# A causal head-wise convolution with a wave token mixing on one NeuronCore: residual adds on GpSimd, conv bands from TensorE, GpSimd in written order, one weight load per matrix and quarter, two-bank PSUM tiles

## The chip, the cores and the metric

The kernel runs on one core of one Trainium2 chip. The engines are named as the profile names them: PE (TensorE, matmul), DVE (VectorE), ACT (ScalarE), POOL (GpSimd) and SP (SyncE). In this kernel POOL and SP issue the DMA transfers. The metric is device microseconds (us) of one launch; less is better.

## The reference

Eight sequences of 4224 tokens with 192 channels. A causal convolution with seven taps, whose weights are a softmax for each of eight heads, is followed by a token mixing with complex weights and a channel mixing; both mixings add residuals.

```
w = softmax(weight, axis=-1)                      # (8 heads, 7 taps)
x = einsum('hk,bskhg->bshg', w, windows(x, 7))    # causal, x is (8, 4224, 192)
theta = x @ w_theta                               # w_theta (192, 192)
zr, zi = x * cos(theta), x * sin(theta)
y = einsum('ts,bsd->btd', w_tok_r, zr) + einsum('ts,bsd->btd', w_tok_i, zi)
u = x + y                                         # w_tok_r, w_tok_i (4224, 4224)
out = u + relu(u @ w_ch)                          # w_ch (192, 192)
```

The token mixing is by far the largest part. The token matrices are read as float32 and used as float16; the output is float32.

## The kernel before

**Token mixing.** The sum over 4224 tokens is cut into 33 chunks of 128 tokens (four quarters of 32 tokens from four places of the sequence, `token` names the place). The output's 33 row tiles of 128 tokens are taken two at a time, 17 units. For each chunk and unit the 2x2 product of (real, imaginary) weights by (cos, sin) parts is done with seven products instead of eight: the weight tiles are called "11", "21" (real part of the first and the second row tile), "12", "22" (imaginary part) and the sums "S1" to "S4"; the data tiles of a chunk are Z11, Z21, Z22 and T1 to T4. These are the matmuls of L394, 22 in a run of eleven chunks, seven runs in a step.

**Steps.** At most eleven chunks are resident in SBUF. A step is one unit with the chunks of that time; there are 58 (steps 0 to 57). Chunks 0 to 10 are made in steps 0 to 4 while the first units begin; each chunk serves 17 steps. In steps 17 to 22 and again in 35 to 40 the eleven resident chunks are replaced one or two at a step; this text calls these the two regroups. A row tile's partial sum goes to DRAM (`part`, L407) after steps that are not its last, and comes back (L334, `load_rows`) in the later ones. Steps 41 to 57 are final for their rows; of these 53 to 57 have fewer chunks and are called late.

**A chunk.** `load_chunk` makes a tile `xw` of inputs with a halo of earlier tokens: four loads on POOL (L177) and two copies from the chunk before on SP (L168). `conv` (L190) multiplies it with `bands`, matrices that hold the softmaxed taps, for a pair of heads a call; ACT copies the result out (L197) and SP stores the convolved x to DRAM as `xs` (L207). Then two `transpose` (six PE transposes L144, one ACT copy L148), four `theta` (PE L135, two ACT sines L226), `product` (DVE L231) and `sums` (DVE L237).

**Weights of a step.** `load_w` loads one named weight tile in four transfers, one a quarter (L289 on POOL), into a staging tile `st` with four buffers. `turn` (L301) transposes blocks of 32 on DVE from `st` to `wt`; `wsum` (L313) makes S1 to S4 on DVE.

**Residual.** `add_x` adds `xs` to the rows of a final step by a POOL transfer that accumulates (L347): into `pv`, the SBUF tile of the rows, or for late steps into `part` in DRAM, four steps ahead. `give` adds a finished run from PSUM to `pv` (ACT L357, DVE L359).

**Output.** `cast` makes a float16 copy `ub` of u on ACT, `turn_u` transposes it, `output` multiplies by w_ch and adds on DVE (L422), and SP stores (L428).

**Order.** `pe`, `dve` and `act` chain the instructions of their engine in the order in which the program writes them. Instructions on POOL and SP are not chained: the framework's scheduler places them. Each step has a list of events with due times in sevenths of the step ("units"); `mix` writes an event out when its matmuls reach that time. In step t: `turn` and `wsum` of step t+1 ("11" at 0.25, "21" 1.2, S3 2.05, "22" 2.2, S1 3.05, S2 3.3, "12" 4.2, S4 5.1), `load_rows` of t+1 at 1.6, `add_x` at 3.3 and 5.0, `load_w` of step t+2 at 0.3, 1.3, 2.3 and 4.3, and in the regroups `load_chunk` at 4.5 for chunks that start at t+2, and the twelve pieces of a chunk that starts at t+1 from 0.3 on (a second chunk 2.6 later).

**Start.** Before the first step POOL makes masks (L502, L504), from which DVE builds `bands` (L541 to L552), loads w_theta (L121 to L124), and issues x and weight loads. `idle` fills PE's early gaps with spare matmuls (L580).

**PSUM.** The tiles `y` of L394 take two banks, in two buffers. All others share the tag `mm`, one bank a tile in four buffers.

Of the kernel before, what the change touches and what calls it, by code (L numbers as in the profile page):

```python
# [10 lines left out]
ALU = mybir.AluOpType  # L11
# [5 lines left out]
def kernel(  # L17
# [69 lines left out]
    def act(ins):  # L87
        return in_order("act", ins)

    constp = ctx.enter_context(tc.tile_pool(name="const", bufs=1))  # L90
# [7 lines left out]
        tc.tile_pool(name="mmps", bufs=4, space=bass.MemoryType.PSUM)  # L98
# [7 lines left out]
    def bank(name, dtype=F32):  # L106
        return mmpool.tile([P, PC if dtype == F32 else 2 * PC], dtype,
                           name=name, tag="mm")
# [6 lines left out]
    ident = constp.tile([P, P], F16, name="ident")  # L115

    def channel_weights(w, name):
        R = D - P
        t = constp.tile([P, 4, D], F16, name=name)
        nc.vector.memset(t[:, 1:3, :], 0.0)  # L120
        nc.gpsimd.dma_start(out=t[:, 0, :], in_=w[0:P, :])  # L121
        nc.gpsimd.dma_start(out=t[0:R, 1, :], in_=w[P:D, :])
        nc.gpsimd.dma_start(out=t[R:P, 2, :], in_=w[0:R, :])
        nc.gpsimd.dma_start(out=t[:, 3, :], in_=w[R:D, :])  # L124
        return t
# [5 lines left out]
    def channel_mix(tT, k, w):  # L131
        v = bank("v")
        for b in range(2):
            for i in range(2):
                pe(nc.tensor.matmul(  # L135
                    v[:, b * D : (b + 1) * D], lhsT=tT[:, 3 * k + b + i, :],
                    rhs=w[:, 2 * b + i, :], start=(i == 0), stop=(i == 1),
                ))
        return v[:, 0 : 2 * D]

    def transposed(u):
        tp = bank("tp", F16)
        for k in range(6):
            pe(nc.tensor.transpose(  # L144
                tp[:, k * P : (k + 1) * P], u[:, k * P : (k + 1) * P], ident
            ))
        uT = wk.tile([P, 6, P], F16, name="uT", tag="uT")
        act(nc.scalar.activation(  # L148
            out=uT[:, :, :].rearrange("p k s -> p (k s)"), in_=tp[:, 0 : 6 * P],
            func=AT.Copy,  # L150
        ))
        return uT
# [3 lines left out]
    class Chunk:  # L156


        def __init__(self, k, before=None):
# [3 lines left out]
            for a in range(NQ):  # L163
# [13 lines left out]
                nc.gpsimd.dma_start(  # L177
                    out=self.xw[lo : lo + n, h, :, :],
                    in_=x[:, t0 : t0 + n, :].rearrange("b s d -> s b d"),
                )  # L180

        def conv(self, hp):
            if hp == 0:
                self.z = zpool.tile([P, 7, HN], F16, name="z", tag="z")
                self.x = self.z[:, T2 : T2 + 2, :].rearrange("p t n -> p (t n)")
            pc = bank("pc")
            for hh in range(2):
                h = 2 * hp + hh
                for half in range(2):
                    pe(nc.tensor.matmul(  # L190
                        pc[half * 2 * Q : (half + 1) * 2 * Q,
                           hh * B * G : (hh + 1) * B * G],
                        lhsT=bands[:, h, :, :].rearrange("p a m -> p (a m)"),
                        rhs=self.xw[:, half, :, h * G : (h + 1) * G],
# [4 lines left out]
                    :, :, hp * 2 * G : (hp + 1) * 2 * G  # L199
                ].rearrange("p b (h g) -> p h b g", h=2),  # L200
                in_=pc[:, 0 : 2 * B * G].rearrange("p (h b g) -> p h b g", h=2, b=B),
                func=AT.Copy,
            ))
            if hp == H // 2 - 1:
# [9 lines left out]
        def theta(self, g, k):  # L214
            v = channel_mix(self.xT[g], k, wth).rearrange(
                "p (b h e) -> p b h e", b=2, h=2
            )
            b0 = g * GB + 2 * k
            for first, bias in ((Z11, half_pi[:]), (Z21, None)):
                o = self.z[:, first : first + 2, :].rearrange(  # L220
                    "p h (b e) -> p b h e", e=HD
                )[:, b0 : b0 + 2, :, :]
# [18 lines left out]
        def tasks(self):  # L241

            for hp in (0, 2):
                yield lambda hp=hp: [self.conv(hp), self.conv(hp + 1)]
            for g in range(NG):
                yield lambda g=g: self.transpose(g)
            for g in range(NG):
                for k in range(2):
                    yield lambda g=g, k=k: self.theta(g, k)
# [17 lines left out]
    class Step:  # L267


        def __init__(self, t):  # L270
# [8 lines left out]
            self.blocks = ("11", "21", "22", "12") if self.pair else ("11", "12")  # L279
            self.st, self.w, self.ub, self.uT, self.pv = {}, {}, {}, {}, []  # L280

        def load_w(self, name):
            tb = self.tbs[int(name[0]) - 1]
            w = (moe_w_tok_r, moe_w_tok_i)[int(name[1]) - 1]
            st = wpool.tile([P, NQ, NW * Q], F16, name="st", tag="st", bufs=4)
            n = self.n * Q
            for a in range(NQ):
                t0 = token(self.ks[0], a)
                nc.gpsimd.dma_start(  # L289
                    out=st[a * Q : (a + 1) * Q, :, 0:n],  # L290
                    in_=w[tb * P : (tb + 1) * P, t0 : t0 + n]
                    .rearrange("(bt i) s -> i bt s", bt=NQ),
                )
            self.st[name] = st
# [4 lines left out]
        def turn(self, name):  # L299
# [3 lines left out]
                self.st[name][:, :, 0 : self.n * Q]  # L303
# [35 lines left out]
        def add_x(self, i):  # L339

            if self.late:
                to = part[(self.t // NU - 1) % 2][self.tbs[i], :, :]
            else:
                to = self.pv[i]
            rows = slice(self.tbs[i] * P, (self.tbs[i] + 1) * P)
            for cols in (slice(0, HN), slice(HN, N)) if self.late else (slice(0, N),):
                nc.gpsimd.dma_start(  # L347
                    out=to[:, cols], in_=xs[rows, cols], accum_op=ALU.add
                )
# [61 lines left out]
        def cast(self, i, g):  # L411
            self.ub[i, g] = wk.tile([P, GC], F16, name="ub", tag="ub", bufs=4)
# [7 lines left out]
        def output(self, i, g, k):  # L420
            pk = self.pv[i][:, g * GC + k * 2 * D : g * GC + (k + 1) * 2 * D]
            dve(nc.vector.scalar_tensor_tensor(  # L422
                out=pk, in0=channel_mix(self.uT[i, g], k, wch), scalar=0.0, in1=pk,
                op0=ALU.max, op1=ALU.add,
            ))
            if k == 1:
                rows = slice(self.tbs[i] * P, (self.tbs[i] + 1) * P)
                nc.sync.dma_start(  # L428
                    out=out[g * GB : (g + 1) * GB, rows, :].rearrange("b s d -> s b d"),
                    in_=self.pv[i][:, g * GC : (g + 1) * GC].rearrange(  # L430
                        "p (b d) -> p b d", d=D
                    ),
                )

        def outputs(self):
# [3 lines left out]
            for i in range(len(self.tbs)):  # L439
                at = ((-self.time / 7 + 0.6, 1.2) if late else (0.7, 12.7))[i]  # L440
                cast, turn, mix = (1, 2.6, 4.4) if late else (2, 3.6, 5.4)
                for g in range(NG):
# [3 lines left out]
                    for k in range(2):  # L446
                        found.append((d + mix + 0.7 * k,
                                      lambda i=i, g=g, k=k: self.output(i, g, k)))
# [8 lines left out]
    def step_events(t):  # L457
# [11 lines left out]
        if t + 2 < NSTEP:  # L469
            nxt = steps[t + 2]  # L470
            for j, name in enumerate(nxt.blocks):
                found.append(((0.3, 1.3, 2.3, 4.3)[j], lambda name=name: nxt.load_w(name)))
# [4 lines left out]
        if t >= NU - 2:  # L477
# [4 lines left out]
            for k in (k for k in range(NK) if start[k] == t + 1 and k >= NW):  # L482
                pos = [0, .5, 1.3, 1.5, 2.1, 2.3, 2.5, 2.7, 3.1, 3.15, 3.4, 3.6]
# [14 lines left out]
    spare = bank("spare")  # L498
    noise = zpool.tile([P, PC], F16, name="noise", tag="z")
    nc.vector.memset(noise, 0.0)  # L500
    masks = wk.tile([2 * WR, KS, 2, Q], F16, name="masks", tag="ub", bufs=4)
    nc.gpsimd.memset(masks, 1.0)  # L502
    for k in range(KS):
        nc.gpsimd.affine_select(  # L504
            out=masks[:, k, :, :], in_=masks[:, k, :, :], pattern=[[WR, 2], [1, Q]],
            channel_multiplier=-1, base=HALO - KS + 1 + k,
            compare_op=ALU.is_equal, fill=0.0,
# [3 lines left out]
    for a, lo in ((0, True), (1, False)):  # L511
# [4 lines left out]
        )  # L516
    wmax = constp.tile([P, H], F32, name="wmax")
# [150 lines left out]
```

## Time and profile before

| what | value |
|---|---|
| median of three runs | 1477.11 us (1475.83 to 1478.19) |
| the profiled execution | 1481.54 us, span 1479.8 us |
| mean granted PE clock | 0.996 |
| PE busy | 1435.6 us (97%) |
| DVE busy | 980.7 us (66%) |
| ACT busy | 385.9 us (26%) |
| POOL busy | 604.5 us (41%) |
| PE idle before L394, most of it for DVE L359 | 24.7 us (19.7) |
| POOL weight issues, L289 | 896 of 0.56 us, 88 KB each |
| POOL x issues, L177 | 132 of 0.594 us, 96 KB each |
| POOL residual issues, L347 | 24 into pv, 0.935 us; 18 into part, 1.217 us |
| moved by DMA | 281.96 MB |

The span is the time between the first and the last instruction of the profiled execution; it is 1.7 us under that execution's own time, which is itself 4.4 us above the median. Busy time of PE counts from the issue of a matmul to its modelled end, so that neighbours overlap: the 7656 matmuls of L394 have a mean of 327 ns each but follow each other about every 161 ns. "Idle before, releaser" is the time an engine stood still before an instruction and what ended it. The granted clock is a share of PE's full clock.

### The profile page before, as it was taken

The page shows a single profiled execution, that of the slowest core. Times are in us where ns is not written, and L with a number is a line of the kernel's source. Part 1 is how long each engine was busy: PE and PEld are TensorE (multiplying, and loading weights), DVE is VectorE, ACT ScalarE, POOL GpSimd, SP SyncE. Part 2 cuts the span into 40 slices and gives each one's busy share as a digit, 9 for nine tenths or more (in the row PEclk, how much of TensorE's full clock was granted, in tenths as well). Part 3 has the DMA queues.
Part 4 walks back from the last instruction along what each step waited for, and adds up shares of the span by engine and source line. Part 5 has one row for each costly group of instructions (what it writes and reads, how often), then busy time and mean ns, then how long its engine had stood idle before and what let it go on. Part 6 is the DMA issues. An engine that isn't in the chain of part 4 may idle for free.

```text
span 1479.8 us, 25342 instructions
## 1 busy us (share of the span) xinstructions
PE 1435.6 (97%) x10083; PEld 902.6 (61%) x10083; DVE 980.7 (66%) x1120; ACT 385.9 (26%) x664; POOL 604.5 (41%) x1096
## 2 busy tenths in 40 slices
PE   6899999999999999999999999998799999999997
PEld 3565666666666666666666666665466666666665
DVE  5885645454558787775666668778476667666676
ACT  5881111111135353000000015254021212222134
POOL 9743424242444542433324254553444333333330
PEclk9999999999999999999999999999999999999999
DMA  9997757464699999887868699999999989998675
GB/s 130 216 206 148 135 99 153 93 148 94 147 226 220 237 216 256 186 195 173 200 163 208 152 199 213 216 286 293 189 233 253 226 206 224 202 218 189 142 170 158
DMA packets 241318, 281.96 MB, mean 191 GB/s; under 512 B 76336, under 2 KB 209456, under 8 KB 241200
## 3 DMA queue, kind: packets, MB, share of 16 engines
q0 software_dynamic: 173280, 111.20, 54.0%
q1 hardware_dynamic: 67920, 169.14, 32.2%
q8 instruction: 79, 1.29, 0.3%
q14 instruction: 39, 0.32, 0.1%
HBM read 245.49 MB, written 108.13 MB: 239 GB/s over the span
## 4 chain that ended last, share of the span: by engine, by line
PE 84%; DMA 9%; POOL 4%; DVE 2%; issue 1%; ACT 0%; SPq 0%; DVEq 0%; POOLq 0%; ACTq 0%
PE y L394 77%; PE v L135 4%; DMA xw<-in_x_dram 3%; DMA st<-in_moe_w_tok_r_dram 3%; PE tp L144 2%; POOL st L289 2%; DMA st<-in_moe_w_tok_i_dram 2%; PE pc L190 1%; DMA part<-xs 1%; POOL xw L177 1%; DVE pv L359 1%; DMA xw<-xw 0%; DMA part<-pv 0%; DVE z L237 0%; DVE z L231 0%
## 5 line engine op out<-in xcount | busy, mean ns | idle before, releaser
L394 PE MATMUL y<-z,wt 128*128 128x384 f16 x7656 | 1312.1, 327 | 24.7 <-DVE pv L359 19.7
L394 PEld LDWEIGHTS <-wt 128*128 128x128 f16 x7656 | 738.1, 98 | 482.7 <-issue 31.5
L359 DVE TENSOR_TENSOR pv<-y,pv 128x768 f32<-128x768 f32 x324 | 308.9, 953 | 429.5 <-PE y L394 414.5
L289 POOL DMA_DIRECT2D st<-in_moe_w_tok_r_dram x448 | 244.2, 566 | 355.0 <-DVE wt L301 302.9
L289 POOL DMA_DIRECT2D st<-in_moe_w_tok_i_dram x448 | 243.7, 562 | 349.6 <-DVE wt L301 296.4
L301 DVE STREAM_TRANSPOSE wt<-st 128x1408 f16<-128x1408 f16 (+7 forms) x224 | 326.6, 1463 | 10.9 <-DMA st<-in_moe_w_tok_r_dram 8.5
L148 ACT ACTIVATE uT<-tp 128x768 f16<-128x768 f16 x132 | 105.5, 817 | 321.8 <-PE tp L144 321.8
L313 DVE TENSOR_TENSOR wt<-wt 128x1408 f16<-128x1408 f16 (+7 forms) x216 | 173.6, 804 | 10.1 <-PE y L394 6.6
L197 ACT ACTIVATE z<-pc 128x384 f16<-128x384 f32 x132 | 58.4, 504 | 384.2 <-PE pc L190 384.0
L357 ACT ACTIVATE pv<-y 128x768 f32<-128x768 f32 x66 | 53.8, 816 | 275.2 <-PE y L394 274.7
L135 PEld LDWEIGHTS <-uT 128*128 128x128 f16 x1056 | 93.4, 98 | 34.9 <-ACT uT L148 3.8
L177 POOL DMA_DIRECT2D xw<-in_x_dram x132 | 76.7, 594 | 50.5 <-DMA st<-in_moe_w_tok_r_dram 18.1
L422 DVE SCALAR_TENSOR_TENSOR pv<-v,pv 128x384 f32<-128x384 f32 x132 | 71.4, 548 | 24.5 <-PE v L135 24.0
L226 ACT ACTIVATE z<-v,half_pi 128x384 f16<-128x384 f32 x132 | 77.7, 589 | 32.3 <-PE v L135 31.2
L237 DVE TENSOR_TENSOR z<-z 128x768 f16<-128x768 f16 x132 | 73.6, 557 | 7.3 <-DMA xs<-z 2.4
L413 ACT ACTIVATE ub<-pv 128x768 f16<-128x768 f32 x66 | 52.2, 835 | 71.8 <-DVE pv L359 71.7
L135 PE MATMUL v<-wch,uT 128*128 128x192 f16 x528 | 63.8, 246 | 2.6 <-ACT uT L148 2.6
L231 DVE TENSOR_TENSOR z<-z 128x1536 f16<-128x1536 f16 x66 | 60.0, 950 | 9.1 <-ACT z L226 9.0
L226 ACT ACTIVATE z<-v 128x384 f16<-128x384 f32 x132 | 65.5, 497 | 0.0
L135 PE MATMUL v<-wth,uT 128*128 128x192 f16 x528 | 62.5, 248 | 0.8 <-ACT z L226 0.8
L347 POOL DMA_DIRECT2D pv<-xs x24 | 22.1, 935 | 71.6 <-ACT ub L413 29.3
L190 PE MATMUL pc<-xw,bands 96*64 96x192 f16 x528 | 35.4, 254 | 4.4 <-DMA xs<-z 1.9
(45 smaller groups left out, 195.3 us busy)
## 6 DMA issues: line engine op xcount, KB each, us to landing
part<-pv SPq DMA_DIRECT2D x79, 768.0 KB, 4.1
pv<-part SPq DMA_DIRECT2D x79, 768.0 KB, 6.5
out_dram<-pv SPq DMA_DIRECT2D x66, 384.0 KB, 4.5
st<-in_moe_w_tok_r_dram POOLq DMA_DIRECT2D x280, 88.0 KB, 5.1
st<-in_moe_w_tok_i_dram POOLq DMA_DIRECT2D x280, 88.0 KB, 3.9
pv<-xs POOLq DMA_DIRECT2D x24, 768.0 KB, 6.8
xs<-z SPq DMA_DIRECT2D x132, 96.0 KB, 4.6
xw<-in_x_dram POOLq DMA_DIRECT2D x121, 96.0 KB, 4.8
```

The lines of the kernel that those rows point to most:

```text
L135: pe(nc.tensor.matmul(v[:, b * D : (b + 1) * D], lhsT=tT[:, 3 * k + b + i, :], rhs=w[:, 2 * b + i, :], start=(i == 0), stop=(i == 1),))
L148: act(nc.scalar.activation(out=uT[:, :, :].rearrange("p k s -> p (k s)"), in_=tp[:, 0 : 6 * P], func=AT.Copy,))
L177: nc.gpsimd.dma_start(out=self.xw[lo : lo + n, h, :, :], in_=x[:, t0 : t0 + n, :].rearrange("b s d -> s b d"),)
L226: act(nc.scalar.activation(**args))
L231: dve(nc.vector.tensor_tensor(out=o, in0=xv, in1=o, op=ALU.mult))
L237: dve(nc.vector.tensor_tensor(out=z[:, o, :], in0=z[:, a, :], in1=z[:, b, :], op=ALU.subtract))
L289: nc.gpsimd.dma_start(out=st[a * Q : (a + 1) * Q, :, 0:n], in_=w[tb * P : (tb + 1) * P, t0 : t0 + n] .rearrange("(bt i) s -> i bt s", bt=NQ),)
L301: dve(nc.vector.transpose(self.w[name][:, 0 : self.n, :, :], self.st[name][:, :, 0 : self.n * Q] .rearrange("p bt (c j) -> p c bt j", j=Q),))
L313: dve(nc.vector.tensor_tensor(out=self.w[name][:, 0 : self.n, :, :], in0=self.w[a][:, 0 : self.n, :, :], in1=self.w[b][:, 0 : self.n, :, : ...
L359: dve(nc.vector.tensor_tensor(out=o, in0=yv, in1=o, op=ALU.add))
L394: pe(nc.tensor.matmul(y[cn][:, q, 0:BH], lhsT=self.w[wn][:, c, :, :].rearrange("p bt i -> p (bt i)"), rhs=chunks[k].z[:, zn, q * BH : (q + ...
L422: dve(nc.vector.scalar_tensor_tensor(out=pk, in0=channel_mix(self.uT[i, g], k, wch), scalar=0.0, in1=pk, op0=ALU.max, op1=ALU.add,))
```

## The change

- `pool()` chains POOL's instructions in written order, as `pe`, `dve` and `act` do: x loads, weight loads, residual adds.
- `load_w` takes one matrix (m=1 real, m=2 imaginary) and loads both row tiles of the step at once: four transfers of twice the size, `st` has twice the size and two buffers. They are filed at 1.3 (real) and 4.3 (imaginary).
- `add_x` of a final step that isn't late loads `xs` into a tile `xr` on SP and adds it to `pv` on GpSimd. For late steps the accumulating transfers remain.
- The tiles of tag `mm` have two banks in two buffers instead of one bank in four. `conv` handles four heads a call (one ACT copy for two before), `theta` half a chunk (two sines for four), `output` half a row tile (one DVE operation for two).
- The conv bands come from 32 small matmuls of a shifted selection matrix by the seven taps, instead of masks and fourteen DVE multiplications and additions.
- w_theta is loaded by SP in float32 and cast on DVE; w_ch stays on POOL, at the end of the start as before. The weights of step 1 are requested before the start's loop instead of in its second turn. Spare matmuls are shorter, and fewer.
- `ub` has two buffers instead of four.

```diff
+    def pool(ins):
+        return in_order("pool", ins)
...
-        tc.tile_pool(name="mmps", bufs=4, space=bass.MemoryType.PSUM)
+        tc.tile_pool(name="mmps", bufs=2, space=bass.MemoryType.PSUM)
...
-    def bank(name, dtype=F32):
-        return mmpool.tile([P, PC if dtype == F32 else 2 * PC], dtype,
+    def banks(name, dtype=F32):
+        return mmpool.tile([P, 2, PC if dtype == F32 else 2 * PC], dtype,
                            name=name, tag="mm")
...
-                nc.gpsimd.dma_start(
+                pool(nc.gpsimd.dma_start(
                     out=self.xw[lo : lo + n, h, :, :],
                     in_=x[:, t0 : t0 + n, :].rearrange("b s d -> s b d"),
-                )
+                ))
...
-        def load_w(self, name):
-            tb = self.tbs[int(name[0]) - 1]
-            w = (moe_w_tok_r, moe_w_tok_i)[int(name[1]) - 1]
-            st = wpool.tile([P, NQ, NW * Q], F16, name="st", tag="st", bufs=4)
-            n = self.n * Q
+        def load_w(self, m):
+            w = (moe_w_tok_r, moe_w_tok_i)[m - 1]
+            st = wpool.tile([P, 2, NQ, NW * Q], F16, name="st", tag="st", bufs=2)
+            n, nb = self.n * Q, len(self.tbs)
             for a in range(NQ):
                 t0 = token(self.ks[0], a)
-                nc.gpsimd.dma_start(
-                    out=st[a * Q : (a + 1) * Q, :, 0:n],
-                    in_=w[tb * P : (tb + 1) * P, t0 : t0 + n]
-                    .rearrange("(bt i) s -> i bt s", bt=NQ),
-                )
-            self.st[name] = st
+                pool(nc.gpsimd.dma_start(
+                    out=st[a * Q : (a + 1) * Q, 0:nb, :, 0:n]
+                    .rearrange("i r bt s -> i (r bt) s"),
+                    in_=w[self.tbs[0] * P : (self.tbs[0] + nb) * P, t0 : t0 + n]
+                    .rearrange("(bt i) s -> i bt s", i=Q),
+                ))
+            self.st[m] = st
...
         def add_x(self, i):
-            if self.late:
-                to = part[(self.t // NU - 1) % 2][self.tbs[i], :, :]
-            else:
-                to = self.pv[i]
             rows = slice(self.tbs[i] * P, (self.tbs[i] + 1) * P)
-            for cols in (slice(0, HN), slice(HN, N)) if self.late else (slice(0, N),):
-                nc.gpsimd.dma_start(
-                    out=to[:, cols], in_=xs[rows, cols], accum_op=ALU.add
-                )
+            if not self.late:
+                xr = wk.tile([P, N], F16, name="xr", tag="xr", bufs=1)
+                nc.sync.dma_start(out=xr, in_=xs[rows, :])
+                pool(nc.gpsimd.tensor_tensor(
+                    out=self.pv[i], in0=self.pv[i], in1=xr, op=ALU.add
+                ))
+                return
+            for cols in (slice(0, HN), slice(HN, N)):
+                pool(nc.gpsimd.dma_start(
+                    out=part[(self.t // NU - 1) % 2][self.tbs[i], :, cols],
+                    in_=xs[rows, cols], accum_op=ALU.add,
+                ))
...
-            self.ub[i, g] = wk.tile([P, GC], F16, name="ub", tag="ub", bufs=4)
+            self.ub[i, g] = wk.tile([P, GC], F16, name="ub", tag="ub", bufs=2)
...
-            for j, name in enumerate(nxt.blocks):
-                found.append(((0.3, 1.3, 2.3, 4.3)[j], lambda name=name: nxt.load_w(name)))
+            for m in (1, 2):
+                found.append((1.3 + 3 * (m - 1), lambda m=m: nxt.load_w(m)))
...
-                pos = [0, .5, 1.3, 1.5, 2.1, 2.3, 2.5, 2.7, 3.1, 3.15, 3.4, 3.6]
+                pos = [0, .5, 1.3, 1.6, 2.1, 2.5, 3.1, 3.15, 3.4, 3.6]
...
+    idle(8)
+    bp = banks("bp")
+    for q in range(Q):
+        pe(nc.tensor.matmul(
+            bp[0 : 2 * WR, 0, q * H : (q + 1) * H],
+            lhsT=sel[:, Q - 1 - q : Q - 1 - q + 2 * WR], rhs=taps,
+            start=True, stop=True,
+        ))
...
-    for name in steps[0].blocks:
-        steps[0].load_w(name)
+    for m in (1, 2):
+        steps[0].load_w(m)
     load_chunk(2)
...
+    for m in (1, 2):
+        steps[1].load_w(m)
     for i in range(NW + 1):
...
-            for name in steps[1].blocks:
-                steps[1].load_w(name)
         if i + 3 < NW:
             load_chunk(i + 3)
```

## The prediction

> **What bounds the kernel now.** I read the page first, then PE's waits, then a table of busy time by stretches of 37 us, and last the timelines of two stretches.
>
> ```profile
> span 1479.8 us, 25342 instructions
> PE 1435.6 (97%) x10083; PEld 902.6 (61%) x10083; DVE 980.7 (66%) x1120; ACT 385.9 (26%) x664; POOL 604.5 (41%) x1096
> POOL 9743424242444542433324254553444333333330
> ...
> L394 PE MATMUL y<-z,wt 128*128 128x384 f16 x7656 | 1312.1, 327 | 24.7 <-DVE pv L359 19.7
> ```
>
> PE is the bound. An undisturbed stretch holds 230 matmuls of L394 in 37 us, a pitch of 0.161 us, so 7656 of them take 1232 us. With 1056 of L135 at 0.0825 (87), 792 transposes of L144 at 0.056 (44) and 528 of L190 at 0.0565 (30), pitches taken in the same way, the useful work is 1393 us of the span of 1479.8. No part of the change alters these counts, so all it can move is the other 87 us. PE's waits name the parts (waited-for, total us, times, longest).
>
> ```profile
> PE y L394 <- DVE pv L359: 19.7, 11, 6.0
> ...
> PE pc L190 <- DMA xw<-in_x_dram: 1.5, 1, 1.5
> ```
>
> Only one conv wait on an x load is there, 1.5 us. The stretches tell where the time lies (start:end and length, then busy us of PE, PEld, DVE, ACT and POOL, granted PE clock, DMA share, GB/s).
>
> ```profile
> 0.00:37.00 37.00, 25.48 (x184) 13.60 (x185) 19.11 (x46) 21.06 (x41) 34.62 (x75) 0.95 0.98 130
> 37.00:74.00 37.00, 30.02 (x281) 19.80 (x279) 31.45 (x49) 31.88 (x66) 28.80 (x53) 1.00 1.21 216
> 481.00:518.00 37.00, 36.35 (x274) 22.95 (x273) 26.59 (x30) 13.39 (x27) 19.73 (x36) 1.00 1.04 237
> 962.00:999.00 37.00, 37.00 (x303) 23.95 (x302) 26.78 (x34) 21.03 (x42) 19.45 (x33) 1.00 1.18 285
> 999.00:1036.00 37.00, 32.86 (x257) 20.98 (x254) 30.28 (x36) 18.11 (x38) 14.29 (x24) 0.98 1.14 293
> 1036.00:1073.00 37.00, 27.93 (x163) 16.16 (x161) 17.44 (x17) 1.66 (x3) 16.84 (x28) 0.93 0.93 188
> 1277.00:1314.00 37.00, 37.00 (x273) 24.52 (x272) 26.55 (x33) 8.55 (x11) 15.71 (x27) 1.00 0.99 227
> ```
>
> Three things are to be seen. The ramp: PE misses 11.5 + 7.0 us in the first two rows and 2.4 in the next 37, with POOL busy 34.6 of the first 37. The middle is full (36.35 in a stretch with conv work), and the last steps are full too (37.00, DVE at 72%). Between 962 and 1073 PE misses 0 + 4.1 + 9.1 = 13.2 us; the clocks of 0.98 and 0.93 add about 3.4 us, two stretches of 3.41 us at half clock, which the clock's record shows from 1034.4 and 1044.6.
>
> **Part 1, the pile-up near 1040 goes: -16.5 us (-12 to -18).** In the timeline (start, duration, idle before and its releaser) step 41's residual add is issued late:
>
> ```profile
> 1037.45 0.91 POOL L347 DMA_DIRECT2D pv<-xs  x1 [2.89 <-DMA st<-in_moe_w_tok_r_dram]
> ...
> 1044.42 0.96 DVE L359 TENSOR_TENSOR pv<-y,pv 128x768 f32<-128x768 f32 x1 [8.92 <-DMA st<-in_moe_w_tok_i_dram]
> ...
> 1045.43 2.90 PE L394 MATMUL y<-z,wt 128*128 128x384 f16 x9 [6.04 <-DVE pv L359]
> ```
>
> L347's accumulating transfer pv<-xs leaves POOL at 1037.45, DVE's `give` waits 8.92 us and PE 6.04. (The releaser named there is another transfer that ended then; pv is what this instruction shares with L347.) POOL is held up since the 18 accumulating transfers into `part` for the late steps, which the code files under steps 49 to 53, were issued at 952.8 to 1014.5: DMA share rises to 1.18 and 1.14. The change gives POOL the written order, so they go out at their own steps, and the pv add becomes a plain 384 KB load on SP plus a GpSimd add. The loss was 13.2 + 3.4 = 16.6; I keep 16.5. At steps 49 to 53 the transfers meet a DMA share of 0.65 to 0.99 and a full PE; there I charge 0 to 3 us, and take 0, as DVE stands idle 10 us of each 37.
>
> **Part 2, the ramp: -8 us (-11 to -3).** POOL issued 32 weight loads of 541 to 566 ns and 4 of theta before x load 4 (out at 36.5 us). Now there are 16, twice as large; the nearest row for more packets is an x load at 594 ns. 32 x 0.566 + 4 x 0.56 - 16 x 0.594 = 10.8 us earlier. Conv 5 starts at 53.1 us; the later convs follow each other by 8 us, set by ACT (31.9 busy of 37) and a DMA share of 1.21, so not all of it gets through. Nothing of it would leave -3 (the POOL time ahead of x load 2 alone, some 5 us, partly covered by the first weight landings); all of it -10.8. I take -8. The bands chain (14 DVE operations, 4.6 us, become 32 tiny matmuls at 0.056 to 0.163, 1.8 to 5.2 us) nets 0 +- 2. The spare matmuls fill waits and count 0.
>
> **Part 3, a new wait on x loads in both regroups: +27 us (+2 to +57).** A chunk's four x loads are filed at 4.5 of a step's 7 units. The weights of a step came as four single loads at 0.3, 1.3, 2.3 and 4.3 with four buffers; now the imaginary half of both row tiles is one load at 4.3 with two buffers, whose old tenant is read last by turn "12", filed at 4.2. So on POOL the order is now: four weight issues that wait for turn "12", then the x loads. Before, with POOL free to be rearranged, x loads of a step's first chunk left 1 to 4 us ahead of the weights (521.15 in the timeline, where turn "12" starts at 523.74). The second chunk's loads already stand where the first's will:
>
> ```profile
> 523.74 1.37 DVE L301 STREAM_TRANSPOSE wt<-st 128x1152 f16<-128x1152 f16 x1
> 525.41 2.15 POOL L289 DMA_DIRECT2D st<-in_moe_w_tok_i_dram  x4 [2.53 <-DVE wt L301]
> 527.56 2.29 POOL L177 DMA_DIRECT2D xw<-in_x_dram  x4
> 532.56 0.52 PE L190 MATMUL pc<-xw,bands 96*64 96x192 f16 x8
> ```
>
> Turn "12" ends at 525.11; four weight issues (2.15 us) and four x issues (2.29) follow, and the last of the x loads landed at 534.77, 9.7 us after the turn. x loads of this stretch (390 to 620 us) take
>
> ```profile
> DMA to landing us min/median/max: 2.9/4.8/8.0
> ```
>
> With 0.2 for wider packets the loads are in 9.9 us after the turn. The first conv of the next step started, after the turn's end, 9.2, 7.4, 7.2, 6.4, 7.5, 7.4 us later in steps 17 to 22 and 9.3, 7.4, 7.3, 6.3, 7.4, 7.3 in steps 35 to 40 (532.56 is one). The differences are 0.7, 2.5, 2.7, 3.5, 2.4, 2.5 and 0.6, 2.5, 2.6, 3.6, 2.5, 2.6: 26.7 us, and PE runs in written order, so all of L394 is queued behind the conv. Nothing hides it: PE is full there. If the last load takes the least landing, 2.9, it is in 7.2 us after the turn and the sum is under 2; with the greatest, 8.0, 12.3 us and 57. I take the measured sequence, 27. What is late next: ACT's copy, the transposes, theta; all come over a unit (3.8 us) ahead of use.
>
> **Part 4, half clock after these waits: +10 us (0 to +20).** In this trace a stretch of 3.41 us in which PE idles more than about 57% is followed by as much at half clock (after the 2.03 us gap at 1034, the 6.04 at 1045); a 2.53 us wait at 66.8 that fell across two stretches was not. A 2.6 us gap at a random phase puts 1.95 us into one stretch 6 times in 10; each costs 1.7 us (3.41 at half speed); 10 x 0.6 x 1.7 = 10. The Trainium skill ("TensorE: Matmul & The Clock Gate", "Why this matters for your kernels") warns only of idle gaps over about 3 us; by it this term would be 0 or 2 us and the time 8 us less. The drop after 2.03 us at 1034 speaks against leaning on it.
>
> **Part 5, the residual add on GpSimd: +1 us (0 to +22).** 24 adds of 128x1536. The trace has no POOL add: memset's slope (0.83 ns a column) gives 1.4 us, affine_select's (269 ns at 64, 390 at 128, 1.9 a column) 3.05. Before, pv<-xs took 0.94 + 6.8 to be in; now a 384 KB SP load (out_dram, the same size, 4.5) and the add, 5.9 to 7.6: no later. DVE's first `give` of the final steps stays covered unless the load takes longer; at 6.5 (SP's 768 KB row) plus 3.05 it is 1.9 us late, x 12 steps = 22. I take 1. The Trainium skill ("SBUF — State Buffer", "Who interferes with whom") says a DVE operation with two SBUF inputs blocks against a GpSimd one that reads SBUF; L313 and L231 are such. No row here shows it.
>
> **Part 6, the rest: 0 (-2 to +6).** Two-bank PSUM tiles merge pairs of ACT and DVE instructions (ACT 26% busy; L422's 548 x 2 becomes about 953, as L359's 128x768); two `mm` buffers for four and two `ub` for four can delay a transpose behind its reader by one ACT copy (0.8 us), in the tail mostly.
>
> **Sum.** 1479.8 - 16.5 - 8 + 27 + 10 + 1 = 1493.3 for the profiled span. That run took 1481.5, 4.4 over the median of the three shown (1477.1), so 1477.1 + 13.5 = 1490.6: I say 1490.
>
> **The rivals.** A, the other side: the x loads are in time. Its place is the first conv of each regroup step; its price is parts 3 and 4 together, 37 us; it decides from 7.3 us: if the loads are in by then, ten of twelve convs wait for nothing. For it: one landing can be 2.9, DVE runs behind PE there and a stall would let it catch up and bring turn "12" forward, and merged loads leave DMA emptier. Against: the measured 9.7. Then 1477.1 - 16.5 - 8 + 1 = 1454, up to 1466 if half of a stall is left. B: the adds come late in the final steps, part 5's 22 us: 1511 with the stalls, 1475 without; DVE's idle 28% there speaks against it. C: the written POOL order doesn't undo the pile-up, as step 41's first residual still has to wait for its landed part rows: 1490 + 16 = 1506 or 1470. D: stalls of about 1 us, no half clock, cancel the gains: 1477.
>
> **How the numbers follow.** Forecast 0.56, A 0.27, B 0.06, C 0.05, D 0.06. The forecast's own range is 1476 (no half clock, 20 us of stalls) to 1508 (landing 1 us later). The whole range reaches down into A, to 1454, and up to 1507; about 0.1 is left below and 0.08 above. 0.2%, 3 us, is about what a measurement tells from no change. Faster: A and the halves of B, C with no stalls, 0.30; same: D and the lower edge of the forecast, 0.08; slower 0.62.
>
> **What would show it.** Part 3: PE's waits name conv <- x loads about ten times with 2 to 4 us, first conv of steps 17 to 22 and 35 to 40, and x issues sit right behind weight issues. Part 4: a clock under 1.00 in those stretches. Part 1: no PE wait on pv between 1020 and 1060. Part 2: conv 5 near 45 us. Part 5: the POOL add's duration, and L313 no longer than its 804 ns. It is wrong if conv waits in the regroups are under 1 us each, or if the final steps lose their 37.00.

## The result

The changed kernel takes 1556.15 us (median of four runs, 1551.32 to 1558.65), the kernel before 1477.65 beside it: a ratio of 1.052, interval 1.0481 to 1.056. It is slower by some 78 us, on the side that was forecast, but outside the range. The profiled execution took 1551.32 us, the shortest of the four; that of the kernel before was 4.4 us above its median, so the two traces differ by less, 69.8 us. The ratios below leave out one execution of after_free_order, which took 2517 us at a mean clock of 0.555.

From the page of the changed kernel come the span, PE's row, the groups of the token matmul and of the conv matmul (busy, mean ns, idle before and its releaser), and the x loads' median time to landing (last column):

```profile
span 1549.6 us, 24465 instructions
PE 1460.6 (94%) x10099; PEld 914.5 (59%) x10099; DVE 1032.8 (67%) x1044; ACT 366.4 (24%) x467; POOL 434.6 (28%) x655
...
L401 PE MATMUL y<-z,wt 128*128 128x384 f16 x7656 | 1315.3, 329 | 13.5 <-DVE pv L366 11.9
...
L193 PE MATMUL pc<-xw,bands 96*64 96x192 f16 x528 | 44.3, 284 | 51.5 <-DMA xw<-in_x_dram 38.8
...
xw<-in_x_dram POOLq DMA_DIRECT2D x121, 96.0 KB, 6.2
```

PE is busy for 94% instead of 97%. The matmul itself is unchanged (329 ns against 327), the idle time before L401 has even shrunk; the new idle time, 51.5 us, stands before the conv, where it was 4.4. An x load lands 6.2 us after its issue in the median, where it took 4.8. PE's waits (waited-for, total us, times, longest):

```profile
PE pc L193 <- DMA xw<-in_x_dram: 38.8, 18, 5.6
PE y L401 <- DVE pv L366: 11.9, 8, 5.2
PE pc L193 <- issue: 10.9, 4, 4.2
```

The third row is the same wait where the profile found no releaser: the longest, 4.2 us, ends with the conv at 522.23, and that conv's second x load landed at 522.14. The stretches, in the columns of the prediction:

```profile
0.00:37.00 37.00, 27.99 (x228) 17.64 (x229) 19.08 (x44) 24.23 (x32) 27.15 (x57) 0.95 1.16 161
37.00:74.00 37.00, 31.28 (x285) 20.90 (x284) 30.94 (x45) 30.01 (x41) 18.69 (x33) 0.95 1.20 247
481.00:518.00 37.00, 31.63 (x201) 18.58 (x199) 22.90 (x29) 6.45 (x8) 8.57 (x16) 0.91 0.68 130
1073.00:1110.00 37.00, 28.41 (x219) 17.89 (x217) 32.04 (x33) 14.06 (x18) 15.39 (x19) 0.98 1.05 252
1277.00:1314.00 37.00, 37.00 (x269) 24.27 (x268) 31.25 (x24) 7.74 (x10) 12.11 (x13) 1.00 0.78 190
```

The stretch 481 to 518, which had been full (36.35), now misses 5.4 us and 9% of the clock. The ramp is only a little fuller (27.99 + 31.28 against 25.48 + 30.02, at a lower clock). The stretch around step 41 (now 1073 to 1110) still misses 8.6 us. The final steps are full as before.

Where the time went can be read more sharply: the beginning of a step in the trace is its first token matmul, and since the steps are the same in both kernels, the stages can be set side by side. Us against the same stage of the kernel before, each from one profiled execution (the runs below the second row are the experiments):

| run | start, to step 5 | steps 17-22 | steps 35-40 | step 41 | step 57 and after |
|---|---|---|---|---|---|
| kernel before, the stage itself | 135.2 | 160.1 | 153.7 | 39.6 | 18.3 |
| the changed kernel | -4.0 | +38.3 | +37.1 | -7.1 | +5.0 |
| w_after_x | -1.8 | +0.3 | +0.3 | -6.6 | +5.8 |
| before_in_order | -0.6 | +24.4 | +17.0 | -4.7 | 0.0 |
| after_free_order | -3.8 | +0.3 | +0.9 | -6.3 | +6.3 |
| dma_residual | -5.2 | +42.0 | +38.4 | -8.7 | +5.6 |
| before_order_x_first | +2.6 | 0.0 | -2.2 | -7.7 | 0.0 |
| x_first_dma_residual | -4.4 | +0.3 | -1.6 | -3.5 | +5.9 |
| x_first_dma_ub4 | -4.2 | +0.3 | -1.6 | -4.3 | +1.5 |
| x_first_dma_ub4_onebank | -6.6 | 0.0 | -2.2 | -3.4 | +0.1 |
| spares_in_wait | -4.7 | +30.0 | +28.4 | -9.3 | +5.6 |
| half_before_x | -1.7 | +29.6 | +33.3 | -7.1 | +5.8 |

All other stages agree within 0.6 us. The row of the changed kernel sums, with 0.4 us of step 56, to 69.7, the difference of the spans but for rounding (1549.6 - 1479.8): the two regroups are the whole loss and more, 75.4 us. How far one execution can be read is seen in the changed kernel and dma_residual, which run the same program in steps 17 to 22 and still differ by 3.7 us there.

The timeline of the changed kernel at the first conv of step 18 (start, duration, idle before and its releaser):

```profile
441.42 1.37 DVE L304 STREAM_TRANSPOSE wt<-st 128x1152 f16<-128x1152 f16 x1
...
443.09 2.28 POOL L291 DMA_DIRECT2D st<-in_moe_w_tok_i_dram  x4 [11.87 <-DVE wt L304]
445.42 2.85 POOL L180 DMA_DIRECT2D xw<-in_x_dram  x5
...
451.48 0.24 PE L193 MATMUL pc<-xw,bands 96*64 96x192 f16 x1 [1.49 <-DMA xw<-in_x_dram]
...
454.33 0.85 PE L193 MATMUL pc<-xw,bands 96*64 96x192 f16 x7 [2.61 <-DMA xw<-in_x_dram]
```

Turn "12" ends at 442.79, the four weight issues follow, and only behind them the x loads. The conv's first matmul waits 1.49 us and its second 2.61 (its sixteen need all four loads); the last load landed at 454.29, 11.5 us after the turn. The same reading gives a median of 11.6 us for the twelve steps (9.6 to 16.1).

### The profile page after: what moved, and what is told of

Read it like the earlier page. It is cut to its first block, busy times and chain, and to the rows that moved or that the text cites. A ratio compares the mean times of both kernels' runs of the same rounds, so it can differ in the third digit from the quotient of the medians.

```text
span 1549.6 us, 24465 instructions
## 1 busy us (share of the span) xinstructions
PE 1460.6 (94%) x10099; PEld 914.5 (59%) x10099; DVE 1032.8 (67%) x1044; ACT 366.4 (24%) x467; POOL 434.6 (28%) x655
## 4 chain that ended last, share of the span: by engine, by line
PE 79%; DMA 8%; DVE 5%; POOL 2%; ACT 2%; issue 2%; SPq 1%; POOLq 0%; DVEq 0%; ACTq 0%
PE y L401 70%; DMA xw<-in_x_dram 6%; PE v L138 4%; PE tp L147 2%; PE pc L193 2%; DMA xs<-z 1%; POOL st L291 1%; DVE wt L304 1%; DVE z L241 1%; DVE pv L366 1%; ACT z L230 1%; POOL xw L180 1%; DVE z L235 1%; ACT z L200 1%; SPq L212 1%
## 5 line engine op out<-in xcount | busy, mean ns | idle before, releaser
L401 PE MATMUL y<-z,wt 128*128 128x384 f16 x7656 | 1315.3, 329 | 13.5 <-DVE pv L366 11.9
L401 PEld LDWEIGHTS <-wt 128*128 128x128 f16 x7656 | 743.5, 99 | 493.8 <-issue 38.6
L291 POOL DMA_DIRECT2D st<-in_moe_w_tok_i_dram x232 | 132.4, 578 | 544.6 <-DVE wt L304 539.1
L291 POOL DMA_DIRECT2D st<-in_moe_w_tok_r_dram x232 | 132.4, 579 | 511.2 <-DVE wt L304 506.6
L316 DVE TENSOR_TENSOR wt<-wt 128x1408 f16<-128x1408 f16 (+7 forms) x216 | 231.4, 1071 | 10.2 <-PE y L401 6.6
L200 ACT ACTIVATE z<-pc 128x768 f16<-128x768 f32 x66 | 53.7, 813 | 456.9 <-PE pc L193 456.8
L193 PE MATMUL pc<-xw,bands 96*64 96x192 f16 x528 | 44.3, 284 | 51.5 <-DMA xw<-in_x_dram 38.8
L430 DVE SCALAR_TENSOR_TENSOR pv<-v,pv 128x768 f32<-128x768 f32 x66 | 62.2, 947 | 26.2 <-PE v L138 23.6
L348 POOL TENSOR_TENSOR pv<-pv,xr 128x1536 f32<-128x1536 f32 x24 | 74.9, 3120 | 6.6 <-PE tp L147 6.4
L193 PEld LDWEIGHTS <-bands 96*64 96x64 f16 x528 | 25.9, 123 | 77.5 <-DMA xw<-in_x_dram 44.6
L230 ACT ACTIVATE z<-v,half_pi 128x768 f16<-128x768 f32 x66 | 59.5, 902 | 40.2 <-PE v L138 40.2
L138 PE MATMUL v<-wch,uT 128*128 128x192 f16 x528 | 54.0, 246 | 4.5 <-ACT uT L151 4.5
```

Source lines behind the costliest of these rows:

```text
L138: pe(nc.tensor.matmul(v[:, k, b * D : (b + 1) * D], lhsT=tT[:, 3 * k + b + i, :], rhs=w[:, 2 * b + i, :], start=(i == 0), stop=(i == 1),))
L193: pe(nc.tensor.matmul(pc[half * 2 * Q : (half + 1) * 2 * Q, h // 2, h % 2 * B * G : (h % 2 + 1) * B * G], lhsT=bands[:, 4 * j + h, :, :].r ...
L230: act(nc.scalar.activation(**args))
L291: pool(nc.gpsimd.dma_start(out=st[a * Q : (a + 1) * Q, 0:nb, :, 0:n] .rearrange("i r bt s -> i (r bt) s"), in_=w[self.tbs[0] * P : (self.t ...
L316: dve(nc.vector.tensor_tensor(out=self.w[name][:, 0 : self.n, :, :], in0=self.w[a][:, 0 : self.n, :, :], in1=self.w[b][:, 0 : self.n, :, : ...
L401: pe(nc.tensor.matmul(y[cn][:, q, 0:BH], lhsT=self.w[wn][:, c, :, :].rearrange("p bt i -> p (bt i)"), rhs=chunks[k].z[:, zn, q * BH : (q + ...
```

## The experiments

**1. Order undone by one number (w_after_x).**

```diff
-                found.append((1.3 + 3 * (m - 1), lambda m=m: nxt.load_w(m)))
+                found.append((1.3 + 3.3 * (m - 1), lambda m=m: nxt.load_w(m)))
```

> The changed kernel, with the imaginary weights of a step filed at 4.6 instead of 4.3, behind the x loads at 4.5; nothing else. Theory (the x loads wait on GpSimd's queue behind weight loads that wait for turn '12'): the first convs of steps 17 to 22 and 35 to 40 wait for nothing, the 6.83 us half-clock stretches in both regroups are gone, and the some 75 us that steps 17 to 22 and 35 to 40 lost (38.3 and 37.1) come back: 1475 to 1490 us. Rival 1 (x loads are slow because the merged weight transfers fill the DMA queue, wherever they stand): landings of x loads stay at 6 us or more, and at least half of the loss stays: over 1515. Rival 2 (pairs of banks in two buffers make the pieces of a chunk wait for each other): conv waits vanish but PE still loses 30 us or more in the regroups: over 1510.

1475.05 us, ratio 0.9968 (0.9955 to 0.998). No conv of the regroups waits, and both are back at +0.3 us. The same place of this run's timeline:

```profile
431.99 2.28 POOL L180 DMA_DIRECT2D xw<-in_x_dram  x4
...
442.21 1.37 DVE L304 STREAM_TRANSPOSE wt<-st 128x1152 f16<-128x1152 f16 x1
...
443.32 2.28 POOL L180 DMA_DIRECT2D xw<-in_x_dram  x4 [9.05 <-PE v L138]
445.59 0.58 POOL L291 DMA_DIRECT2D st<-in_moe_w_tok_i_dram  x1
...
450.69 0.52 PE L193 MATMUL pc<-xw,bands 96*64 96x192 f16 x8
```

The four x loads of the chunk that this conv reads leave at 431.99, 10 us before turn "12" begins, and the last of them landed at 441.53; the conv starts with no wait. The four at 443.32 belong to the step's second chunk; they too leave ahead of the weights. x loads still take a median of 6.1 us to land between 390 and 1010 us, so rival 1 had the landings right, yet they cost nothing, as there is time. The pairs of banks (rival 2) cost nothing here either. That 0.3 of a unit is worth 75 us is shown.

**2. The order alone, in the kernel before (before_in_order).**

```diff
-                nc.gpsimd.dma_start(
+                pool(nc.gpsimd.dma_start(
```

at L177, L289 and L347.

> The kernel before, with GpSimd's x loads, weight loads and residual transfers chained in written order; four weight loads a step, one bank a tile and everything else as before. Theory: the written order alone makes the wait, since the fourth weight load of a step stands at 4.3, ahead of the x loads at 4.5: conv waits of 2 to 4.5 us in the regroups, 40 to 80 us lost there; the accumulating transfers into DRAM leave their place before step 41, so 7 to 16 us come back there: 1505 to 1545 us. Rival 1 (the merged loads make the x loads late, not the order): the regroups lose under 10 us, the time is 1455 to 1475. Rival 2 (two-bank tiles): the same, 1455 to 1475.

1518.19 us, ratio 1.0254 (1.0231 to 1.0276). PE's waits of this run:

```profile
PE pc L193 <- DMA xw<-in_x_dram: 25.2, 11, 5.3
...
PE pc L193 <- issue: 3.8, 3, 1.9
```

The written order is enough to make the wait: 24.4 + 17.0 = 41.4 us in the regroups, in ten of the twelve steps, and 4.7 us back at step 41. So 34 of the 75 us need something else of the change. Step 41 gained less than the 7 to 16 us expected.

**3. The changed kernel without the order (after_free_order).**

```diff
     def pool(ins):
-        return in_order("pool", ins)
+        return ins
```

> The changed kernel without the chain on GpSimd: the scheduler places x loads, weight loads and residual work as in the kernel before. Theory: x loads come out ahead of the waiting weight loads in most of the regroup steps; conv waits under 1 us in at least 8 of 12 steps, but the accumulating transfers into DRAM are issued early again, so the loss of some 16 us around step 41 is back: 1470 to 1505 us. Rival 1 (merged loads): conv waits of 4 us stay, over 1530. Rival 2 (two-bank tiles): over 1520 with no conv waits.

1478.79 us, ratio 0.999 (0.9979 to 1.0001). No conv waits in the regroups: with merged loads but a free order nothing is lost there. Half of the expectation failed: the accumulating transfers into `part` are issued early again, from 939 us on, nine of them before step 41 begins, yet step 41 still gains 6.3 us.

**4. The order in the kernel before, x loads first (before_order_x_first).**

```diff
-                found.append(((0.3, 1.3, 2.3, 4.3)[j], lambda name=name: nxt.load_w(name)))
+                found.append(((0.3, 1.3, 2.3, 4.6)[j], lambda name=name: nxt.load_w(name)))
```

> The kernel before with GpSimd chained in written order and its fourth weight load filed at 4.6 instead of 4.3, behind the x loads at 4.5. Theory: against the run with the order alone, the 41 us of steps 17 to 22 and 35 to 40 come back, and the gain at step 41 (some 5 to 8 us) stays: a ratio to the kernel before of 0.993 to 0.997, 1468 to 1475 us. Rival (the chain of GpSimd itself costs, by queues that can no longer be rearranged): conv waits are gone but the regroups keep 10 us or more: 1485 or more.

1473.9 us, ratio 0.9955 (0.994 to 0.997), as expected: with experiment 2 it shows the order to be free where what is needed next doesn't stand behind a head that waits.

**5. Half of the bytes ahead of the x loads (half_before_x).** The changed kernel, with the imaginary load split by row tile (`load_half`, not shown, issues the four transfers of one row tile):

```diff
-            for m in (1, 2):
-                found.append((1.3 + 3 * (m - 1), lambda m=m: nxt.load_w(m)))
+            found.append((1.3, lambda: nxt.load_w(1)))
+            for r in range(len(nxt.tbs)):
+                found.append((4.3 + 0.3 * r, lambda r=r: nxt.load_half(r)))
```

> The changed kernel with the imaginary weights as two loads of half the size, one for each row tile: the first stays at 4.3, ahead of the x loads at 4.5, the second is filed at 4.6, behind them. Theory (the x loads wait for turn '12', and land the later the more weight bytes are queued ahead of them): the wait stays, but the last x load lands 10 to 10.7 us after the turn instead of 11.4 to 12; conv waits of 2 to 3.5 us, and the regroups lose 35 to 50 us as in the kernel before with the written order (41): 1510 to 1530 us. Rival 1 (bytes ahead don't matter, the 34 us between 41 and 75 come from the larger tiles or the pairs of banks): 1545 to 1560. Rival 2 (half the wait is gone at once, as for the x loads behind everything): under 1490.

1538.95 us, ratio 1.0402 (1.0381 to 1.0423): between the theory and rival 1. The last x load lands mostly 10.1 to 11.4 us after the turn (a median of 10.5, against 10.4 in experiment 2 and 11.6 in the changed kernel), and the regroups lose 29.6 + 33.3 = 62.9 us. The bytes ahead thus account for some 12.5 of the 34 us. Part of the rest is that all twelve steps lose time here, and ten in experiment 2 (41.4 / 10 = 4.1 us each, against 62.9 / 12 = 5.2); why the other two are let off was not tried.

**6. PE kept busy in the wait (spares_in_wait).** 26 matmuls that compute nothing, before the first conv of each regroup step of the changed kernel:

```diff
+            if j == 0 and self.k >= NW and self.k % NW in (0, 2, 4, 5, 7, 9):
+                for _ in range(26):
+                    pe(nc.tensor.matmul(pc[:, 0, 0:BH], lhsT=ident, ...))
```

> The changed kernel with 26 spare matmuls of 128x384 (4.2 us at 0.161) before the first conv of each step of both regroups, into the PSUM tile that the conv then overwrites; the x loads stay behind the weight loads. Theory: PE waited 4.0 to 6 us there, and the 6.83 us of half clock that follow cost some 25 us of the 75; with PE busy in the wait the clock stays at 1.00 in most of the twelve steps and the conv waits shrink to under 1 us: the regroups lose 45 to 58 us, the time is 1525 to 1540 us. Rival (the wait alone costs the 75 us, the clock's record is a shadow of it): the spares run in time that is lost anyway, the regroups lose 70 us or more: 1550 to 1565.

1537.64 us, ratio 1.0398 (1.0374 to 1.0421). Three stretches, of the changed kernel first (its row of 481 to 518 stands above) and then of this run, in the same columns:

```profile
444.00:481.00 37.00, 32.90 (x239) 20.41 (x237) 24.42 (x30) 14.53 (x19) 12.15 (x22) 0.91 0.96 204
518.00:555.00 37.00, 28.90 (x216) 18.07 (x215) 22.03 (x28) 12.79 (x16) 10.28 (x18) 0.91 0.91 193
```

```profile
444.00:481.00 37.00, 37.00 (x287) 23.90 (x286) 27.21 (x33) 15.97 (x20) 13.66 (x24) 1.00 0.96 207
481.00:518.00 37.00, 35.79 (x244) 21.94 (x243) 23.64 (x29) 6.44 (x8) 9.13 (x16) 1.00 0.77 155
518.00:555.00 37.00, 34.75 (x271) 21.75 (x270) 22.15 (x27) 13.58 (x17) 9.11 (x16) 1.00 0.98 207
```

The clock is 1.00, where the changed kernel had 0.91 in each of these. The regroups lose 58.4 us (at the theory's upper edge). The spares were busy for 52.7 us and 7.1 us of conv waits are left; these make 59.8, so with the clock at 1.00 nothing is lost beyond spares and waits. In the changed kernel the waits come to 38.8 + 10.9 = 49.7 us, and 75.4 - 49.7 = 25.7 us are lost beyond them: that is the price of the half clock. The run gets back only 75.4 - 58.4 = 17 of it, since the spares and the waits that are left take some 10 us more than the waits did. The wait itself is the greater part.

**7. The residual by DMA, in the changed kernel (dma_residual).**

```diff
-                xr = wk.tile([P, N], F16, name="xr", tag="xr", bufs=1)
-                nc.sync.dma_start(out=xr, in_=xs[rows, :])
-                pool(nc.gpsimd.tensor_tensor(
-                    out=self.pv[i], in0=self.pv[i], in1=xr, op=ALU.add
-                ))
+                pool(nc.gpsimd.dma_start(
+                    out=self.pv[i], in_=xs[rows, :], accum_op=ALU.add
+                ))
```

> The changed kernel, but the residual of final steps comes by the accumulating transfer into pv on GpSimd's queue in written order, as in the kernel before, instead of a load and a GpSimd add. Theory: the add is what makes DVE's sums of weights slow in the final steps (1311 ns for 128x1408 against 886 before) and what delays the first final step; DVE's mean is back under 950 ns, and the 5.2 us wait near step 41 with its half-clock stretch shrinks: 1543 to 1556, 0 to 10 us less than the changed kernel. Rival (the loss at step 41 comes from part rows and their landings, whoever adds): the same time within 3 us, or 5 to 10 us more, as the transfers take POOL's queue.

1556.65 us, ratio 1.0519 (1.0503 to 1.0534): the rival's "same time". But DVE's rows show the add's effect. DVE's sums of weights in the changed kernel, and then in this run (busy us, mean ns of one):

```profile
L316 DVE TENSOR_TENSOR wt<-wt 128x1408 f16<-128x1408 f16 x136 | 178.2, 1311 | 7.0 <-PE y L401 5.1
```

```profile
L316 DVE TENSOR_TENSOR wt<-wt 128x1408 f16<-128x1408 f16 x136 | 120.4, 886 | 7.0 <-PE y L399 5.1
```

The sums take 1311 ns instead of 886: (1311 - 886) x 136 = 58 us of DVE time are lost beside the GpSimd adds. PE doesn't feel it, for in both runs the final steps keep their distance to the kernel before. DVE had the room.

**8. The residual by DMA, x loads first (x_first_dma_residual).** Experiments 1 and 7 together.

> The changed kernel with the imaginary weights behind the x loads (4.6) and the residual as an accumulating transfer into pv on GpSimd's queue, without the GpSimd add. Theory: in the run with the x loads first the step 41 still loses about 4 us and the one before 2, since DVE's products (4.98 us for two that take 1.82 alone) stand still beside a GpSimd add of 3.11 us, so that DVE's addition to pv comes late and PE waits 1.8 and 5.2 us and falls to half clock at 1033.9; without the add these waits are under 2 us together and step 41 takes 29 to 31 us: 3 to 6 us less than with the add, 1469 to 1473. Rival (the part rows or the residual arrive late, whoever adds): steps 40 and 41 lose as much or more, 1475 to 1485.

1478.1 us, ratio 0.9989 (0.9978 to 1.0): the rival. Against w_after_x, what the step before 41 gains (1.9 us) step 41 more than gives back (3.1). First the changed kernel's timeline at that place:

```profile
1100.27 4.98 DVE L235 TENSOR_TENSOR z<-z 128x1536 f16<-128x1536 f16 x2
1101.31 3.10 POOL L348 TENSOR_TENSOR pv<-pv,xr 128x1536 f32<-128x1536 f32 x1
...
1107.54 0.95 DVE L366 TENSOR_TENSOR pv<-y,pv 128x768 f32<-128x768 f32 x1
...
1108.54 3.76 PE L401 MATMUL y<-z,wt 128*128 128x384 f16 x12 [5.20 <-DVE pv L366]
```

Two products of DVE take 4.98 us beside a GpSimd add of 3.10 us; the addition to pv comes late, and PE waits 5.20. Now this run:

```profile
1023.89 0.98 POOL L346 DMA_DIRECT2D pv<-xs  x1
...
1040.43 0.96 DVE L364 TENSOR_TENSOR pv<-y,pv 128x768 f32<-128x768 f32 x1 [8.60 <-issue]
...
1041.44 8.74 PE L399 MATMUL y<-z,wt 128*128 128x384 f16 x35 [6.19 <-DVE pv L364]
```

The products are quick again. The residual of step 41's second row tile is issued at 1023.89, but it landed only at 1040.35, after 16.5 us, the longest of this run's 24 (median 11.1); DVE's addition follows it at once, having waited 8.60 us, and PE waits 6.19. The partial rows of that tile had landed at 1016.36, before the issue. One wait has taken the other's place: the rows of the first final step are ready too late either way. Why this transfer took so long was not tried.

**9. Four ub buffers (x_first_dma_ub4).**

```diff
-            self.ub[i, g] = wk.tile([P, GC], F16, name="ub", tag="ub", bufs=2)
+            self.ub[i, g] = wk.tile([P, GC], F16, name="ub", tag="ub", bufs=4)
```

> The same as x_first_dma_residual, with four ub buffers instead of two. Theory: in the last 24 us ACT's casts wait for PE's transposes because only two ub are there (2.7, 1.3, 3.2 us before a cast), PE waits in turn and falls to half clock at 1464 and 1474; four ub take 2 to 4 of the 5.8 us that the tail lost against the kernel before. Rival (the pairs of banks make it: a transpose waits for DVE's addition to free a pair, 0.4 to 0.8 us each): under 1.5 us come back.

1475.75 us, ratio 0.9971 (0.9957 to 0.9986). The tail falls from +5.9 to +1.5 us, a little more than was expected. What it removed is seen in the tail of w_after_x, with two buffers:

```profile
1466.32 0.80 PE L147 MATMUL tp<-ident,ub 128*128 128x128 f16 x6
...
1467.21 0.84 ACT L420 ACTIVATE ub<-pv 128x768 f16<-128x768 f32 x1 [2.72 <-PE tp L147]
...
1467.96 1.49 ACT L151 ACTIVATE uT<-tp 128x768 f16<-128x768 f16 x2
...
1468.81 1.53 PE L138 MATMUL v<-wch,uT 128*128 128x192 f16 x16 [0.79 <-ACT uT L151]
```

ACT's cast waits 2.72 us until PE's transpose has read the older ub, ACT's copy uT comes after the cast, and PE's v waits for uT. PE, DVE and ACT take turns.

**10. One bank a tile (x_first_dma_ub4_onebank).** `conv`, `theta`, `output` and their PSUM tiles as in the kernel before; order with x loads first, merged loads, DMA residual and the new start stay.

> The same as x_first_dma_ub4, with the tiles of tag mm as one bank in four buffers, and conv, theta and output in the smaller pieces of the kernel before; order, merged weight loads and start stay those of the changed kernel. Theory: the pairs of banks cost 6.1 us of PE waits on ACT's sines in the first 111 us and the rest of the tail's loss; without them the tail takes 18 to 20 us after step 57 begins and the start gains 2 to 4 us more: 3 to 6 us less than with pairs, 1462 to 1468, the fastest of all. Rival (pairs are free, since ACT and DVE save instructions): the same within 2 us or slower.

1469.98 us, ratio 0.9934 (0.9919 to 0.9949), 5.8 us under the run with pairs and the fastest of all, though 2 us above the figure expected. The start gains 2.4 us and the tail 1.4. In the run with pairs PE waited, by the waits:

```profile
PE tp L147 <- ACT z L230: 6.4, 10, 1.3
PE v L138 <- ACT z L230: 3.3, 4, 1.0
```

With one bank the first of these is gone and the second 1.6 us. With two buffers, a transpose needs the pair that the sines of the half chunk before still read; with four, there is another bank.

## Why the prediction was wrong

The direction, the mechanism and its place were right: the x loads queued behind weight loads that wait for turn "12", at the first convs of both regroups. Its sizes were not. Of the traces' 69.8 us it forecast 13.5; the parts that follow make up the rest.

- **Part 3, +27, is the step that failed.** The waits came to 49.7 us (38.8 + 10.9). The convs stood where the prediction had them, some 7.2 us after the turn, but the last x load came a median of 11.6 us after it and not 9.9. The 9.9 was one measured sequence (9.7) behind weight loads of half the bytes, and 0.2 us was added for the rest. With loads of that size the median is 10.4 (before_in_order) and with half the bytes ahead 10.5 (half_before_x), so some 1.1 of the missing 1.7 us go with the bytes ahead, and the rest is that one sequence was taken for twelve. x loads of the regroups took a median of 6.6 us instead of 4.8. 12 x 1.7 us is 20 of the 23 missing; another 2 are a slip, for the twelve differences of the prediction sum to 28.7 and not 26.7. The part's own upper end, 57, held it; the whole range did not carry that end and allowed for one microsecond only.
- **Part 4, +10, was too small as a consequence.** It counted gaps of 2.6 us that drop the clock 6 times in 10. In nine of the twelve steps the two gaps before the conv's first and second matmul came to 4 us or more together; in the clock's record these nine show 6.83 us at half clock, and one more step, with a gap of 2.25 us, 3.41; what the clock cost beyond the waits came to 25.7 us (experiment 6). The page of the Trainium skill on the clock gate, "TensorE: Matmul & The Clock Gate" ("Why this matters for your kernels"), warns of idle gaps over about 3 us. The traces don't bear out such a limit for a single gap: in before_in_order gaps of 2.16, 2.25 and 2.78 us were followed by 3.41 us at half clock and one of 2.59 was not, and in the kernel before one of 3.04 us, at 1053, was not either. The prediction was right not to lean on it.
- **Part 1, -16.5, gave -7.1.** Step 41 still waits, for another reason: in the changed kernel PE's 5.20 us stand behind DVE's products, which a GpSimd add delays, and with transfers in place of the add behind a late landing (experiment 8). That the early accumulating transfers were the cause is doubtful: after_free_order has nine of them before step 41 again, and gains nearly as much. The prediction also misread them, for only twelve of the 18 were issued at 952.8 to 1014.0, and six at 1096 to 1118. The order alone (before_order_x_first, -7.7) and the other changes without it (after_free_order, -6.3) each give about as much; which property they share is open.
- **Part 2, -8, gave -4.0.** x load 4 was out at 25.2 us instead of 36.6, 11.4 us earlier where the sum had 10.8, but conv 5 started only 3.7 us earlier, at 49.4 and not near 45. The pairs of banks took 2.4 us (experiment 10), and half-clock stretches fall differently in each execution: runs with the same start gave -1.7 to -5.2.
- **Part 5, +1.** The add took 3.10 us, beside an estimate of 1.4 to 3.05. "SBUF — State Buffer" ("Who interferes with whom") in the Trainium skill was right that DVE's two-input operations contend with it: the sums of weights took 1311 ns against 886, and over all widths 1071 where the prediction looked for no more than 804. It cost nothing in the final steps after step 41, as the prediction had it.
- **Part 6, 0 (-2 to +6).** +5.0 in the tail and 0.4 in step 56. Measured in runs whose tail lost 5.9, the two ub buffers make 4.4 of it (experiment 9) and the pairs of banks 1.4 (experiment 10).

Rival A is refuted, and rival B for the final steps after step 41. Of C the outcome held for a part, since step 41 gave less than half of what was forecast, but not its cause: PE's wait did not end with landed part rows. D didn't occur.

## What to carry to other kernels

A queue that is put into written order waits with its head: before chaining it, list what stands behind each instruction that can wait, and file what is needed soonest ahead of it. One due time moved by 0.3 units was worth 75 us here. A landing time measured behind few bytes is a lower end behind twice as many, and an upper end found for one term belongs in the whole range.

## What was not expected

The half-clock stretches come in multiples of 3.41 us, and in the changed kernel each of the nine regroup steps with waits of 4 us or more cost two of them; 27.31 us, eight times 3.41, lie between the end of one and the start of the next in eight places. Cut into stretches of 3.41 us on that raster, the twelve traces (from 60 us to step 57) show what decides: of the stretches at full clock, 53 in which PE stood idle for 57.9% or more were followed by half clock, none with 56.0% or less was, and one of 58.8% (the kernel before, at 1051) is the only exception. The prediction had read about 57% from one trace. So it counts where a gap falls: the one of 2.59 us at 927 in before_in_order had 51.7% in its fullest stretch, that of 2.25 us at 1048 had 65.8%. And 58 us of DVE time lost to the GpSimd adds left PE's steps 42 to 55 untouched to 0.1 us.
